# u of two tiles in one buffer of 640 columns, channel product with 64-row tails, new order of all work

## The chip, the cores and the metric

The kernel runs on one core of one Trainium2 chip. Five engines share its work: TensorE (PE in the profile, its weight loads PEld), VectorE (DVE), ScalarE (ACT), GpSimd (POOL) and SyncE (SP), which here only issues DMAs. The metric is the device time in microseconds (us), median of several runs. The profile is one execution, with its own time.

## The reference

Two layers. The first is a recurrence over 768 steps, for 4 batches of 8 heads with a state of 40 x 40 each; the second mixes its output over tokens and channels. Cut to what matters:

```python
for t in range(S):                                   # r, k, v, w, a, b: (4, 8, 768, 40)
    y[:, :, t] = einsum('bhd,bhde->bhe', r_t, state)
    Sa = einsum('bhde,bhe->bhd', state, a_t)
    state = state * w_t[:, :, None, :] - einsum('bhd,bhe->bhde', Sa, b_t) \
            + einsum('bhd,bhe->bhde', v_t, k_t)
x = y.transpose(0, 2, 1, 3).reshape(4, 768, 320)
theta = x @ w_theta                                  # (320, 320)
y = einsum('ts,bsd->btd', w_tok_r, x * cos(theta)) + einsum('ts,bsd->btd', w_tok_i, x * sin(theta))
u = x + y
out = u + maximum(u @ w_ch, 0)
```

## The kernel before, in words

The 768 tokens of a batch are six chunks of 128, so there are 24 tiles, 0 to 23, each of 128 tokens by 320 columns (8 heads of 40). Inside a tile the recurrence is done in closed form with products on PE; a state (`gt`) goes from tile to tile of a batch. Heads are padded from 40 to 64 columns, so that two heads fill 128 rows and a score product uses 64 rows of the array for each.

All work is written out by hand in a string, `ORDER`. An entry is a step, its tile, the engine that does it (A is ACT, V is DVE, G is POOL, S is a crossbar transpose by a DMA that SP issues) and, behind @, the PSUM place that it takes. `keep` holds each engine and queue to that order, so the string sets the order of PE, of each other engine, and of the DMAs of SP and POOL. The steps that the text speaks of:

- Loads: `LDW`, `LDR` (w and r of two tiles, 320 KB each), `LDK`, `LDB`, `LDA`, `LDV` (160 KB each), `LDT` (a row block of a token matrix, 192 KB), `LDC` (w_theta and w_ch).
- Decay: `LN` takes the logarithm of w of two tiles; `CSI` and `CSE` sum it over tokens with four 64-row products each, 320 wide (`pair_inc`, `pair_exc`); `CSE` goes on with nine small products for the totals. `INVW` and `WI` take the exponentials. `KH` and `AH` multiply k, b and a with them (tiles `kb`, `ah`).
- `TRK`, `TRA`, `TRR`, `TRV`, `NUT`, `GD` transpose on PE (`sm<-ident,...`), and `EKBT`, `EAT`, `ERT`, `EVT`, `ENUT`, `EGD` copy the result out of PSUM.
- Scores `PSI`, `PHI`, `LV`, `LU`: eight products of 64 rows each (`sc<-...`); `EPSI`, `EPHI`, `ELV`, `ELU` copy them with a mask on DVE, or without one on ACT, where POOL then masks (`MPSI` and so on).
- `X0`, `ENX`, `NU`, `ENU` solve for the tile's inner part; `GT`, `EGT` make the new state (`EGA` adds the old one on DVE, or `GI` does on PE); `Y`, `EX` make x.
- Second layer: `XT`, `EXT` transpose x (three chunks of 128 columns; x has 320, so the buffer of a tile is 384 wide with 64 columns of zeros), or `EXT:..S` does it with the crossbar; `TH` is three products with w_theta, `ETH` copies theta out where it is not read from PSUM, `SIN` takes both functions, `ZR` multiplies with x. `YR:i.j` adds the two token products of tile j of the batch to the sum of tile i. `EU` adds x, which gives u; `UT`, `EUT` transpose u in the same way as x; `CH` is three products with w_ch; `EO` takes max and adds u; `ST` stores.

PE's 3,266 products go through `mm` (line 278) and `transpose` (line 282), so these two lines, with the tiles' names, tell the steps apart in the profile. Copies go through line 270 (ACT) and line 272, products of two tiles through line 275. `EU` is line 705 and `EO` line 715. The first loads of tiles 0 and 1 that are marked A (`LDK:0A LDA:0A LDB:1A LDV:0A`) are issued by ACT's queue, the others by SP's; `LDT` and `LDC` by POOL's.

Of the kernel before, what the change touches and what calls it, by code (L numbers as in the profile page):

```python
# [10 lines left out]
FP32 = mybir.dt.float32  # L11
# [20 lines left out]
TRA:4@0 ELV:3A LDK:5 NU:3 TRK:4@3 LDB:5 GD:1@2 EAT:4V ENU:3A MLV:2G XT:0@0 EKBT:4V CR:4A GT:3@1
GI:3 EGD:1V EGT:3V PSI:4@1 EPSI:4V CV:4G PHI:4@0 LN:6A TRR:4@3 EPHI:4A NUT:3@2 MLV:3G Y:2@1
ENUT:3V LDB:6 LDA:6 AH:5G LDK:6 CSI:6@1 X0:4@2 EX:2V EXT:0A ERT:4A INVW:6A TRV:4@0 ENX:4V
MPHI:4G LDV:5 KH:5G LU:3@0 ERT:5A XT:1@1 NU:4 ELU:3V EXT:1A CSE:6@1 LDV:6 LDT:1.1G ENU:4A
TRA:5@3 WI:6A NUT:4@1 EVT:4V ENUT:4A TRK:5@2 LDK:7 EAT:5V AH:6G XT:2@0 EKBT:5V LV:4@0 TH:0@3
ELV:4V KH:6G PSI:5@1 GD:2@1 LDR:6 SIN:0A TH:1@2 LU:4@0 CV:5G GT:4@3 GI:4 EXT:2A EPSI:5V CV:6G
# [24 lines left out]
XT:7@2 EXT:7A LDB:14 LDT:3.1G ENX:11V TRA:12@3 LU:10@0 LV:11@1 ELU:10V NU:11 GD:9@0 EAT:12A
MLV:10G YR:1.0@2 ELV:11A LDA:14 TH:7@3 ENU:11V PSI:12@0 ETH:7A EGD:9V PHI:12@1 LDT:3.0G EPSI:12V
NUT:11@1 CV:12G KH:13G ENUT:11V YR:1.1 YR:1.2 SIN:7A WT:5.1@0 EPHI:12V YR:1.3 YR:1.4 X0:12@3
ENX:12A YR:1.5 MLV:11G EU:1V CR:12A Y:10@1 LDC:0.3G NU:12 EX:10V LU:11@0 LDK:14 AH:13G EWT:5.1V
SIN:6A TRV:12@2 TRR:12@1 ELU:11V EVT:12A TRK:13@0 EKBT:13V ERT:12A LDT:4.1G TH:8@2 ERT:13A
CSI:14@1 ZR:6G LDV:14 SIN:8A LV:12@0 LDW:16 YR:2.0@1 ELV:12V YR:2.1 TRA:13@0 EAT:13V CV:13G
# [6 lines left out]
LDV:15 NUT:13@3 EPSI:14V TRV:14@1 ENUT:13A CH:1@0 KH:15G EPHI:14A EO:1V TRR:14@2 TH:9@3 EVT:14V
ST:1 ERT:14V ETH:9A TH:10@0 AH:15G GT:13@1 LDR:16 MPHI:14G ETH:10A EGA:13V LDK:16 WT:4.0@3
EGT:13V EWT:4.0V LV:14@0 LU:13@1 TRK:15@0 EKBT:15V EGD:12S SIN:9A Y:12@1 YR:4.0@3 ELV:14V YR:4.1
YR:4.2 YR:4.3 LDT:5.0G ERT:15A TRA:15@0 CV:15G LDA:16 X0:14@2 ELU:13A YR:4.4 EAT:15V ENX:14V
YR:4.5 EU:4V SIN:10A XT:11@0 EXT:11V EX:12V PSI:15@0 MLU:13G PHI:15@1 EPSI:15A NU:14 TRV:15@3
LDB:16 UT:2@0 MPSI:15G EPHI:15V ENU:14A TH:11@1 LDW:18 CSE:16@0 EVT:15A LDV:16 EUT:2V GT:14@2
CSI:16@1 SIN:11A ZR:9G CR:16G CH:2@3 WT:5.0@0 EGA:14V EGT:14V Y:13@1 EO:2V ST:2 EWT:5.0V X0:15@2  # L80
ENX:15V NUT:14@3 WI:16A AH:16G EX:13V YR:5.0@0 YR:5.1 INVW:16A KH:16G YR:5.2 ENUT:14V LDK:17
NU:15 ENU:15V LV:15@0 LU:14@1 ELU:14V LN:18A TRA:16@1 EAT:16A UT:3@3 YR:5.3 LDB:17 LDA:17
NUT:15@2 CV:16G ZR:10G YR:5.4 EVT:16S ENUT:15V YR:5.5 TRK:16@1 EUT:3A EU:5V UT:4@3 CH:3@2
EKBT:16V TRR:16@0 EO:3V GD:13@1 EGD:13V KH:17G ELV:15A LDB:18 PHI:16@1 EPHI:16V PSI:16@0 EUT:4A
ST:3 GT:15@3 EPSI:16A MPSI:16G CH:4@2 LDV:17 Y:14@1 CSE:18@1 LDR:18 EO:4V ERT:16A EX:14V LDK:21
ERT:17A WI:18A TRK:17@2 EGA:15V EGT:15V AH:17G XT:13@1 UT:5@0 LV:16@0 EKBT:17A LU:15@1 EUT:5V
EXT:13V ZR:11G ST:4 ELU:15V X0:16@3 TRA:17@0 CH:5@1 YR:6.0@2 YR:6.1 ENX:16A ELV:16A NU:16 CV:17A
LDK:18 EAT:17V CSI:18@1 YR:6.2 ENU:16V LDA:18 XT:12@0 MLV:15G YR:6.3 EXT:12V EO:5V INVW:18A
PSI:17@0 PHI:17@1 EPSI:17A LDK:19 YR:6.4 GD:14@3 EPHI:17V TH:12@0 EGD:14A NUT:16@1 ENUT:16V ST:5
ETH:12A YR:6.5 LDV:18 MPSI:17G TRV:17@3 GT:16@0 EVT:17V Y:15@1 KH:18G EGA:16V LDA:19 SIN:12A  # L90
LV:17@0 EGT:16V LU:16@1 EX:15V EU:6V XT:14@3 EXT:14A AH:18G LDV:19 X0:17@0 TH:13@1 ENX:17A
MLV:16G LDW:20 TRK:18@2 LDB:19 SIN:13A YR:7.0@3 ELV:17V YR:7.1 YR:7.2 LDK:23 ELU:16V EKBT:18A
CV:18G TH:14@1 SIN:14A CR:18G YR:7.3 YR:7.4 TRA:18@2 YR:7.5 ZR:13G NU:17 ENU:17A EAT:18V
# [43 lines left out]
def kernel(  # L137
# [110 lines left out]
    def rows(p):  # L248
        return slice(64 * p, 64 * p + 64)
# [584 lines left out]
```

## Time and profile before

| what | us |
|---|---|
| median of 3 runs | 207.43 |
| lowest, highest | 206.94, 208.84 |
| time of the profiled execution | 206.92 |
| its span | 205.2 |
| first product of PE starts at | 6.20 |

The span runs from the first instruction to the last one's end. An instruction's row gives its start, its length, its engine and line, what it writes and reads, and how many were merged into the row; in square brackets stands how long its engine had been idle and what ended that. A group's row gives a count and a mean length in ns. Products on PE overlap: a row's length is a product's whole passage, and the distance between the starts of two rows is what PE spends on one.

### The profile page before, as it was taken

What the parts mean: (1) busy time and instruction counts of PE and PEld (TensorE: products, weight loads), DVE (VectorE), ACT (ScalarE), POOL (GpSimd) and SP (SyncE); (2) the same over time, 40 slices, a digit from 0 to 9 for tenths busy, and PEclk for the clock granted to TensorE, in tenths of its full rate; (3) what the DMA queues carried; (4) which work ended last, traced back from release to release, by engine and by line L of the source; (5) the groups of instructions that cost most, each with busy time, mean ns of one, the idle gap of its engine ahead of it and who ended that gap; (6) DMA issues with size and microseconds to landing.
All of it is one profiled execution on the core that took longest, in us unless ns stands there. A gap on an engine that the chain in (4) does not pass through costs nothing.

```text
span 205.2 us, 7809 instructions
## 1 busy us (share of the span) xinstructions
PE 190.1 (93%) x3266; PEld 147.5 (72%) x3266; DVE 170.6 (83%) x334; ACT 154.3 (75%) x259; POOL 147.1 (72%) x157
## 2 busy tenths in 40 slices
PE   0389999999999999999999999999999999999992
PEld 0166777877777887887887877887877787777671
DVE  7256899999999997999799998989888797975653
ACT  2367799997989997999899788987898685822100
POOL 8225778899989699998966886993989785634000
PEclk9999999999999999999999999999999999999999
DMA  7999999998898999899489989987979996433342
GB/s 136 187 240 159 225 171 178 173 230 140 153 221 154 213 159 216 164 213 226 103 171 193 192 172 238 192 135 161 169 97 154 218 129 140 99 90 103 102 150 96
DMA packets 144802, 34.17 MB, mean 167 GB/s; under 512 B 139520, under 2 KB 144768, under 8 KB 144768
## 3 DMA queue, kind: packets, MB, share of 16 engines
q1 hardware_dynamic: 138176, 30.26, 76.5%
q0 software_dynamic: 2432, 2.77, 8.4%
q10 hardware_dynamic: 4160, 0.66, 2.2%
q8 instruction: 25, 0.41, 0.9%
q14 instruction: 9, 0.07, 0.1%
HBM read 29.13 MB, written 3.93 MB: 161 GB/s over the span
## 4 chain that ended last, share of the span: by engine, by line
PE 80%; ACT 6%; DVE 5%; issue 2%; ACTq 2%; POOL 2%; POOLq 0%; DVEq 0%
PE sm L278 39%; PE sc L278 22%; PE sm L282 20%; ACTq L331 1%; ACT kbT L270 1%; ACT psi L270 1%; DVE phi L275 1%; ACTq L326 1%; ACT Wi_two L412 1%; ACT lw_two L338 1%; POOL z L275 1%; DVE lamu L275 1%; DVE rvT L272 1%; POOL lamv L554 1%; POOL phi L554 1%
## 5 line engine op out<-in xcount | busy, mean ns | idle before, releaser
L275 POOL TENSOR_TENSOR kb<-raw_kb,invW_two 128x640 bf16<-128x640 f32 x22 | 33.9, 1542 | 5.5 <-ACT invW_two L373 3.6
L275 POOL TENSOR_TENSOR z<-cs,x 128x640 bf16<-128x640 f32 x22 | 30.8, 1403 | 5.3 <-ACT cs L677 5.3
L278 PE MATMUL sm<-z,wtok_r 128*128 128x320 bf16 x120 | 34.3, 299 | 0.0
L278 PE MATMUL sm<-z,wtok_i 128*128 128x320 bf16 x120 | 34.2, 299 | 0.0
L275 POOL TENSOR_TENSOR ah<-raw_a,Wi_two 128x320 bf16<-128x320 f32 x22 | 19.0, 866 | 8.5 <-issue 5.2
L275 DVE TENSOR_TENSOR psi<-sc,mask_p 128x1024 bf16<-128x1024 f32 x16 | 19.5, 1219 | 1.0 <-PE sc L278 0.9
L554 POOL TENSOR_SCALAR_AFFINE_SELECT psi<-psi 128x1024 bf16<-128x1024 bf16 x8 | 8.7, 1093 | 14.0 <-ACT psi L270 11.6
L275 DVE TENSOR_TENSOR phi<-sc,mask_p 128x1024 bf16<-128x1024 f32 x14 | 17.1, 1219 | 1.6 <-PE sc L278 1.4
L278 PE MATMUL sc<-aT,kbT 64*128 64x128 bf16 x384 | 17.3, 225 | 1.1 <-ACT kbT L270 0.7
L275 DVE TENSOR_TENSOR lamu<-sc,mask_p 128x1024 bf16<-128x1024 f32 x14 | 17.1, 1220 | 0.6 <-PE sc L278 0.3
L282 PE MATMUL sm<-ident,kb 128*128 128x128 bf16 x184 | 14.9, 227 | 2.6 <-DVE kb L275 2.3
L278 PEld LDWEIGHTS <-wtok_r 128*128 128x128 bf16 x144 | 14.0, 97 | 4.6 <-issue 0.3
L270 ACT COPY rvT<-sm 128x512 bf16<-128x512 bf16 x28 | 15.9, 593 | 1.3 <-PE sm L282 0.7
L278 PEld LDWEIGHTS <-wtok_i 128*128 128x128 bf16 x144 | 14.1, 98 | 3.9 <-issue 0.2
L275 DVE TENSOR_TENSOR lamv<-sc,mask_p 128x1024 bf16<-128x1024 f32 x13 | 15.9, 1220 | 1.0 <-PE sc L278 0.5
L677 ACT ACTIVATE cs<-sm 128x320 f32<-128x320 f32 x26 | 9.9, 452 | 8.5 <-PE sm L278 8.4
L278 PEld LDWEIGHTS <-kbT 64*128 64x128 bf16 x384 | 11.9, 97 | 5.8 <-issue 2.4
L278 PEld LDWEIGHTS <-rvT 64*128 64x128 bf16 (+1 forms) x272 | 13.6, 95 | 2.9 <-issue 0.5
L278 PE MATMUL sm<-kb,lamv 128*128 128x40 bf16 x192 | 15.0, 180 | 0.0
L278 PE MATMUL sm<-kb,lamu 128*128 128x40 bf16 x192 | 14.9, 179 | 0.0
L282 PEld LDWEIGHTS <-kb 128*128 128x128 bf16 x184 | 11.5, 101 | 4.2 <-DVE kb L275 2.3
L554 POOL TENSOR_SCALAR_AFFINE_SELECT lamu<-lamu 128x1024 bf16<-128x1024 bf16 x10 | 10.9, 1090 | 4.1 <-ACT lamu L270 4.1
(137 smaller groups left out, 625.0 us busy)
## 6 DMA issues: line engine op xcount, KB each, us to landing
raw_w_two<-in_w_dram SPq DMA_DIRECT2D x12, 320.0 KB, 4.8
raw_r_two<-in_r_dram SPq DMA_DIRECT2D x12, 320.0 KB, 4.8
out_dram<-oo SPq DMA_DIRECT2D x24, 160.0 KB, 2.5
raw_kb<-in_b_dram SPq DMA_DIRECT2D x23, 160.0 KB, 4.6
raw_a<-in_a_dram SPq DMA_DIRECT2D x23, 160.0 KB, 4.5
raw_kb<-in_k_dram SPq DMA_DIRECT2D x23, 160.0 KB, 4.3
raw_v<-in_v_dram SPq DMA_DIRECT2D x23, 160.0 KB, 4.7
wtok_row<-in_moe_w_tok_r_dram POOLq DMA_DIRECT2D x6, 192.0 KB, 4.8
```

Source lines behind the costliest of these rows:

```text
L270: keep(nc.scalar.copy(out=out, in_=in_))
L272: keep(eng[e].tensor_copy(out=out, in_=in_))
L275: keep(eng[e].tensor_tensor(out=out, in0=in0, in1=in1, op=ALU.mult))
L278: keep(nc.tensor.matmul(out, lhsT=lhsT, rhs=rhs, start=start, stop=stop, skip_group_check=True))
L282: keep(nc.tensor.transpose(out=out, in_=in_, identity=ident))
L326: keep(queue[e].dma_start(out=tiles[i].raw_kb[:, j], in_=source(ap, i)))
L331: keep(queue[e].dma_start(out=t, in_=source(ap, i)))
L338: keep(nc.scalar.activation(out=q.lw[:, :, :, 0:D], in_=q.raw_w.rearrange("p h (j d) -> p j h d", j=2), func=AF.Ln))
L412: keep(nc.scalar.activation(out=two, in_=q.cse[:, LO:LO + 2 * DM + 16], func=AF.Exp))
L554: keep(nc.gpsimd.affine_select(out=flat, in_=flat, compare_op=ALU.is_ge, fill=0.0, base=-1, pattern=[[0, 2 * G], [1, 128]], channel_multip ...
L677: keep(nc.scalar.activation(out=cs[i % 5][:, c], in_=tiles[i].theta, func=AF.Sin, bias=(math.pi / 2, 0.0)[c]))
```

## The change

Five things change.

1. u of an even tile and of the next odd one lie in one buffer, 640 columns wide (`u_two`, three of them). The even tile's `UT` takes the chunks of columns 0 to 256 (two), the odd tile's those of 256 to 640 (three); the middle chunk has the last 64 columns of the even u and the first 64 of the odd u. The crossbar transposes two and three chunks likewise.
2. `CH` of a tile has two full products; the third, of 64 rows, goes to a step of its own, `CHR`, done once for a pair: rows 0 to 64 of the shared chunk end the even tile's sum, rows 64 to 128 begin the odd tile's. w_ch is held a second time, shifted by 64 rows (`wch` of five chunks instead of three), which takes two more loads, and `LDC` has new numbers. All 24 tiles are paired so. The code could pair x in the same way (`THR`), but the order has no such step.
3. `CST`, the nine small products for the totals, is a step of its own and no longer the end of `CSE`.
4. x lies in six buffers for two tiles each, still with its zeros; theta has three places instead of four; no load is issued by ACT.
5. The whole order is another one. Which engine does a copy changes in places; counts change from 14 to 15 `UT` on PE and 10 to 9 by the crossbar, 19 to 16 `XT` on PE and 5 to 8 by the crossbar, 11 to 12 `WT` on PE, 5 to 7 `GI` with 11 to 9 `EGA`.

The core of the diff; of the order only its first and last lines:

```diff
-LDW:0 LDK:0A LDB:0 LDA:0A LDA:1 LDB:1A LDK:1 LDV:0A LN:0A LDC:0.0G LDT:0.0G CSI:0@0 LDC:0.1G CSE:0@1 WI:0A
-INVW:0A KH:0V TRK:0@0 AH:0V EKBT:0A TRA:0@3 LDW:2 EAT:0V LDR:0 KH:1V PHI:0@1 PSI:0@0
...
-YR:21.4 YR:21.5 ST:19 CH:20@1 EU:21V YR:22.5 EO:20V YR:23.1 UT:21@0 EUT:21V ST:20 YR:23.2
-YR:23.3 YR:23.4 YR:23.5 EU:22V UT:22@1 CH:21@0 EU:23V EUT:22A EO:21V UT:23@3 CH:22@2 EUT:23V
-CH:23@1 EO:22V ST:21 EO:23V ST:22 ST:23
+LDW:2 LDT:0.0G LDW:0 LDB:0 LDC:0.0G LDT:0.1G LDK:0 LDK:1 LDT:1.0G LDC:0.2G LN:2A CSI:2@0 LDA:0
+LN:0A INVW:2A CSE:0@1 CST:0 CSI:0@0 INVW:0A WI:0A LDB:1 CSE:2@0 CST:2 KH:0V LDA:1 TRK:0@0
+EKBT:0A LDV:0 LDA:2 AH:0V TRA:0@3 LDK:2 KH:1V LDB:2 WI:2A EAT:0V PSI:0@1 AH:1V TRA:1@1 TRK:1@2
+CV:0A LDR:0 EPSI:0V EKBT:1A PHI:0@0 TRV:0@0 EAT:1V LDV:1 AH:2G X0:0@3 ENX:0A EPHI:0V PSI:1@1
+LDV:2 EPSI:1A PHI:1@0 NU:0 LDW:4 KH:2G EPHI:1V ENU:0A TRA:2@1 EAT:2A GT:0@2 EGT:0V EVT:0A LDK:3
+MPSI:1G CR:0A TRK:2@3 CV:1A GD:0@1 LDA:3 TRR:0@0 EKBT:2V ERT:0V PHI:2@1 LDB:3 X0:1@2 EPHI:2V
...
+LU:23@1 ELU:23V YR:17.2 YR:17.3 EUT:14S YR:17.4 Y:22@0 EUT:15S EX:22V YR:19.1 YR:17.5 YR:18.2
+EU:17V TH:21@1 EXT:22S Y:23@3 CH:14@0 ETH:21V EX:23V SIN:21A YR:19.2 YR:23.0@2 EXT:23S YR:23.1
+CHR:15@1 EO:14V CH:15 ZR:21G YR:20.0@1 EUT:17S YR:21.0 YR:21.1 TH:22@3 EO:15V YR:19.3 SIN:22A
+ZR:22G TH:23@0 YR:21.2 EUT:16S YR:23.2 ETH:23V YR:22.0@1 ST:14 YR:18.3 SIN:23A YR:20.1 YR:20.2
...
+YR:22.4 ST:19 YR:22.5 EO:18V UT:21@0 YR:23.4 EU:22V ST:18 YR:23.5 EUT:21A CH:20@3 CHR:21@1
+EU:23V UT:22@0 EO:20V UT:23@2 EUT:22V ST:20 CH:21 EUT:23V EO:21V ST:21 CH:22@3 CHR:23@0 EO:22V
+ST:22 CH:23 EO:23V ST:23
...
-    x_t = padded("x", [128, 3 * 128], 2 * NCH, lambda t: t[:, DM:])
-    u_t = padded("u", [128, 3 * 128], 3, lambda t: t[:, DM:])
+    u_two = [consts.tile([128, 2 * DM], BF16, name=f"u_two_{n}") for n in range(3 if twin_u else 0)]
+    def home(i, twins, one, two):
+        if i not in twins:
+            t = one[i % len(one)]
+            return t[:, 0:DM], t
+        t = two[i // 2 % len(two)]
+        if i % 2:
+            return t[:, DM:2 * DM], t[:, 256:2 * DM]
+        return t[:, 0:DM], t[:, 0:256]
...
-    th = mw.tile([128, 4, DM], FP32, name="th")
+    th = mw.tile([128, 3, DM], FP32, name="th")
-    wch = mw.tile([128, 3, DM], BF16, name="wch")
+    wch = mw.tile([128, 5 if twin_u else 3, DM], BF16, name="wch")
...
-        for kt in range(3):
+        for kt in range(src.shape[1] // 128):
             transpose(pt[:, kt * 128:kt * 128 + 128], src[:, kt * 128:kt * 128 + 128])
...
+    def mix(i, b, name, lhs, rhs, twins):
+        q = tiles[i]
+        if i not in twins:
+            setattr(q, name, bank(b))
+            for kt in range(3):
+                mm(getattr(q, name)[:, 0:DM], lhs[:, kt, :], rhs[:, kt, :], kt == 0, kt == 2)
+        elif i % 2 == 0:
+            setattr(q, name, bank(b))
+            for kt in range(2):
+                mm(getattr(q, name)[:, 0:DM], lhs[:, kt, :], rhs[:, kt, :], kt == 0, False)
+        else:
+            for kt in range(2):
+                mm(getattr(q, name)[:, 0:DM], lhs[:, 1 + kt, :], rhs[:, 3 + kt, :], False, kt == 1)
+
+    def mix_ends(i, b, name, lhs, rhs):
+        setattr(tiles[i], name, bank(b))
+        for c in range(2):
+            mm(getattr(tiles[i - 1 + c], name)[:, 0:DM], lhs[rows(c), 0, :], rhs[rows(c), 2, :],
+               c == 1, c == 0)
...
     def chan(i, b):
         q = tiles[i]
-        q.ops = bank(b)
-        mix3(q.ops[:, 0:DM], q.uT, wch)
+        mix(i, b, "ops", q.uT, wch, twin_u)
...
     def weight_load(n):
-        dst, src = ((wth, moe_w_theta), (wch, moe_w_ch))[n // 2]
+        dst, src = ((wth, moe_w_theta), (wch, moe_w_ch))[n // 4]
+        first, part = n % 2, n % 4 // 2
+        if part == 0:
+            keep(nc.gpsimd.dma_start(
+                out=dst[:, 3 * first:3 * first + 2, :],
+                in_=src[64 * first:64 * first + 256, :].rearrange("(a p) d -> p a d", p=128)))
+        else:
+            keep(nc.gpsimd.dma_start(out=dst[rows(first), 2, :],
+                                     in_=src[256 * (1 - first):256 * (1 - first) + 64, :]))
```

More of the change, by code (lines that the diff above doesn't have):

```diff
@@ L32 @@
[L32 to L37, printed above, removed]
@@ L62 @@
[L62 to L67, printed above, removed]
@@ L74 @@
[L74 to L91, printed above, removed]
```

260 lines of the change are left out of this document (145 added, 115 removed).

## The prediction

> **What bounds the kernel now.** I read the page first, then the stretches of 10 us, the waits of PE, and a piece of PE's own order.
>
> ```profile
> span 205.2 us, 7809 instructions
> PE 190.1 (93%) x3266; PEld 147.5 (72%) x3266; DVE 170.6 (83%) x334; ACT 154.3 (75%) x259; POOL 147.1 (72%) x157
> PE   0389999999999999999999999999999999999992
> PEclk9999999999999999999999999999999999999999
> PE 80%; ACT 6%; DVE 5%; issue 2%; ACTq 2%; POOL 2%; POOLq 0%; DVEq 0%
> ```
>
> PE is busy 93% of the span and carries 80% of the chain that ended last. It is idle only at the two ends, and the granted clock shows no loss. The stretches and PE's waits say the same:
>
> ```profile
> 0.00:10.00 10.00, 1.59 (x17) 0.90 (x17) 5.05 (x47) 3.33 (x4) 5.53 (x17) 1.00 1.05 161
> 10.00:20.00 10.00, 8.71 (x100) 6.69 (x100) 5.82 (x10) 7.03 (x11) 3.72 (x3) 1.00 1.20 207
> 20.00:30.00 10.00, 9.38 (x198) 7.22 (x194) 8.78 (x13) 7.92 (x13) 6.98 (x9) 1.00 1.01 197
> 40.00:50.00 10.00, 9.85 (x200) 7.98 (x198) 9.89 (x17) 9.51 (x18) 9.55 (x12) 1.00 0.95 181
> 100.00:110.00 10.00, 10.00 (x170) 8.15 (x164) 9.63 (x17) 9.28 (x16) 7.25 (x9) 1.00 0.79 151
> ```
>
> ```profile
> PE sc L278 <- ACT lw_two L338: 6.5, 2, 6.2
> PE sm L282 <- DVE kb L275: 2.3, 1, 2.3
> ```
>
> Columns of the stretches: length, busy time of PE, PEld, DVE, ACT and POOL, granted clock, DMA share, GB/s. From 40 us on PE is full, so there a product that goes is time gained; between 40 and 50 us DVE, ACT and POOL are nearly full too, so an eviction added there would cost. Before 30 us PE waits, for the first logarithm and for the first kb, and runs slowly: 100 instructions in its second stretch, 198 in the third. There the loads and the chain of the first tiles decide.
>
> **What a product costs PE.** A busy row shows a product's whole passage. What it costs in a full PE is the time until the next one starts, which a piece of PE's order shows:
>
> ```profile
> 109.53 0.30 PE L278 MATMUL sm<-z,wtok_r 128*128 128x320 bf16 x1
> 109.67 0.30 PE L278 MATMUL sm<-z,wtok_i 128*128 128x320 bf16 x1
> 109.81 0.33 PE L282 MATMUL sm<-ident,x 128*128 128x128 bf16 x3
> 110.07 0.62 PE L278 MATMUL sc<-aT,kbT 64*128 64x128 bf16 x16
> 110.62 0.37 PE L278 MATMUL sm<-nx,phi 128*128 128x40 bf16 x8
> ...
> 111.06 0.33 PE L282 MATMUL sm<-ident,u 128*128 128x128 bf16 x3
> 111.22 0.57 PE L278 MATMUL sm<-wth,xT 128*128 128x320 bf16 x3
> 111.73 0.45 PE L278 MATMUL sc<-lw_two,pair_exc 64*128 64x320 bf16 x4
> 112.11 0.18 PE L278 MATMUL sc<-off_two,ident 128*128 128x16 bf16 x1
> ```
>
> A product 320 wide takes 0.14 (109.53 to 109.67), a transpose 0.053 (three from 111.06 to 111.22). The three theta products should be through at 111.22 + 3 x 0.135 = 111.63, but the 64-row products behind them start at 111.73: going over to 64 rows costs 0.10. The four 64-row products, 320 wide, are followed at 112.11, 0.38 later: two pairs side by side (2 x 0.135) and 0.11 for going back. So a lone visit to 64 rows costs about 0.2 for its two changes, and a pair of tails another 0.135. The Trainium skill says the same of the change ("TensorEngine Tiling (Array Packing)", Key Properties: "Mode switching requires drain", changing the tiling mode drains TensorE). By that rule alone, with every tail a lone visit, a pair of tails would cost 0.34 against 0.27 for the two full products that it replaces, a loss of about 0.8 us over 12 pairs; the trace agrees with the drain.
>
> **What PE's list loses and gains** (counted in the two orders, entry by entry). Channel product: 72 products become 48 full ones and 12 pairs of tails, 72 x 0.1355 = 9.8 before, 48 x 0.1355 + 12 x 0.133 = 8.1 after: -1.7. Transposes of u on PE 42 to 39, of x 57 to 48, of the token rows 66 to 72: -6 x 0.055 = -0.3. The product that adds the old state (GI) 5 to 7: +0.3. Changes between 128 and 64 rows: 167 before, 153 after, though 12 tails came in. Seven of the 12 CHR stand beside other 64-row products, and CST, split from CSE, lets CSE and CSI stand together. -14 x 0.10 = -1.4. In all -3.1 us of PE's time, none of it hidden by other work. Up to the end of the last token product (YR:23.5) it is -3.5, because more channel work is left for the end.
>
> **The end.**
>
> ```profile
> 199.35 0.30 PE L278 MATMUL sm<-z,wtok_i 128*128 128x320 bf16 x1
> 199.69 0.49 DVE L705 TENSOR_TENSOR u<-sm,x 128x320 bf16<-128x320 f32 x1 [0.33 <-PE sm L278]
> 200.67 0.35 DVE L272 COPY uT<-sm 128x384 bf16<-128x384 bf16 x1
> 201.69 0.49 DVE L715 SCALAR_TENSOR_TENSOR oo<-sm,u 128x320 f32<-128x320 f32 x1
> ```
>
> The last token product is through at T = 199.35 + 0.14 = 199.49; the last output (EO:23) starts on DVE at T + 2.2. After the change DVE has EU:23, EO:20, EUT:22, EUT:23 one after another: T + 0.2 + 0.49 + 0.49 + 0.35 + 0.35 = T + 1.88. Then PE does the tails of 22 and 23 (CHR:23, which waits for uT of 23), two changes and two products of CH:23, while EO:22, which cannot start before CHR:23 has closed its sum, is queued on DVE ahead of EO:23: tails through at T + 2.2, EO:22 T + 2.4 to 2.9, EO:23 at T + 2.9. That is +0.7.
>
> **Late crossbar transposes.** The crossbar transposes x eight times now (five before) and u nine times (ten).
>
> ```profile
> xT<-x SPq DMA_TRANSPOSE x4, 3.2
> ```
>
> That is the median from issue to landing in us, from 120 us on. The chain Y:23, EX:23, EXT:23, TH:23 went over PE; now EXT:23 goes over SP's queue. Between Y:23 and TH:23 lie 3.2 us of PE's work; the chain needs 0.2 + 0.49 + 3.2 = 3.9. +0.6 or 0.7 is late, bounds 0 (other stalls ahead give the time) and 2 (two transposes queued ahead on SP, and behind them EUT:17 and EUT:16, which CH:17 and CH:16 wait for). I take +0.6.
>
> **The head.** Before, tile 0's w goes first, and four loads of tiles 0 and 1 go by ACT's queue. After, all go by SP's, w of tile 2 ahead of w of tile 0, and three token rows by POOL's instead of one.
>
> ```profile
> GB/s 0 0 0 0 17 87 184 288 285 261 240 231 184 179 183 182 181 184 180 181 184 203 189 199 196 195 198 215 281 286 296 305 278 262 236 214 186 168 177 168
> ```
>
> ```profile
> 5.41 0.74 ACT L338 ACTIVATE lw_two<-raw_w_two 128x640 bf16<-128x640 f32 x1 [3.33 <-DMA raw_w_two<-in_w_dram]
> 9.17 0.83 DVE L275 TENSOR_TENSOR kb<-raw_kb,invW_two 128x640 bf16<-128x640 f32 x1 [3.76 <-ACT invW_two L373]
> 10.05 1.04 PE L282 MATMUL sm<-ident,kb 128*128 128x128 bf16 x8 [2.26 <-DVE kb L275]
> 17.31 0.63 SPq L331 DMA_DIRECT2D raw_a<-in_a_dram  x1
> 23.95 0.86 POOL L275 TENSOR_TENSOR ah<-raw_a,Wi_two 128x320 bf16<-128x320 f32 x1
> ```
>
> The first line is the rate in slices of 0.4 us from the start. The two w are 655 KB; at 285 from about 2.3 us on they have landed by 4.7, so LN:0 can start near 5.0, though LN:2 is ahead of it on ACT, and everything behind up to the first kb keeps its lengths: near 8.6 instead of 9.17, -0.5 (bounds -1, if the four w-sums of both tiles are out of the way before PE is wanted, and +0.7, LN:2's length, if w of 0 lands late). The prices come later: tile 3's last input is 864 KB (0.88 MB) further back, at the 197 GB/s of the third stretch 4.5 us. Its cover: a of tile 3 was issued at 17.31 and is wanted at 23.95; with the page's median landing
>
> ```profile
> raw_a<-in_a_dram SPq DMA_DIRECT2D x23, 160.0 KB, 4.5
> ```
>
> it lay ready 2.1 us, and TRK:3 stands 2.1 us of PE's work later in the new list. 4.5 - 4.2 leaves +0.3, bounds 0 and 4.5.
>
> **The other engines.** DVE has 289 entries with an operand of its own in both orders, ACT 221 and 220, POOL 143 and 146 (a z, a mask, a cast and two weight loads more, two casts of v fewer), against 35, 51 and 58 us that they have free. In the first 50 us of PE's work, where the row of 40 to 50 us shows no free DVE, DVE has 86 entries instead of 89, so I cost the moves at nothing; three more there would be 1.5 us, since PE follows DVE in that stretch. The two added loads of w_ch (200 KB, 1 us of DMA at 197) go by POOL's queue long before the first CH. The theta buffer has three places instead of four, and in the list each is read by SIN before ETH writes it again.
>
> **The sum.** 205.2 - 3.5 + 0.7 + 0.6 - 0.5 + 0.3 = 202.8 of span. The profiled execution took 206.92, 1.7 more than its span, and lay 0.5 under the median of 207.43: 202.8 + 1.7 + 0.5 = 205.0.
>
> **Rivals.**
> *The head starves, slower.* One cause, the order of the loads: w of tile 0 lands late behind w of tile 2 (+0.7 instead of -0.5), and the 4.5 us by which tile 3's inputs come later lie on the path whole: 205.0 + 1.2 + 4.2 = 210.4. For it: the DMA share stands at 1.0 or above in each stretch to 30 us, so nothing can catch up. Against it: PE's waits name no DMA, and the new list has TRK:3 2.1 us later. From 2.4 us of such waits on nothing is gained, from 4.5 on it is slower by over 1%. 0.14.
> *The gain goes into the new waits, no change.* Two crossbar transposes queue ahead of EXT:23 and EUT:16 (+2 instead of 0.6), and three evictions come late where DVE is full, half of their 1.5 us hidden: 205.0 + 1.4 + 0.7 = 207.1. For it: those engines are full. Against it: a count of all places where a result is wanted by PE within half a us of its earliest end gives 75 in the old order and 77 in the new after 20 us, so the new list is no tighter. 0.14.
> *The tails don't run side by side.* Then each pair takes 0.27: +1.6, 206.6. Against it: the four 64-row products above, 0.38 with a change. 0.03.
> *PE starts and warms earlier.* The eight transposes at 10.05 take 1.04; at 0.053 apart they would take 0.6 (seven steps and the last one's passage of 0.22): the early products run at about half rate. The first w-sums may start when the first w is in, some 1.5 us sooner than now; if all behind follows by that much instead of 0.5, and the fast rate saves another 1.0, 203.0. The Trainium skill has this rule ("TensorE: Matmul & The Clock Gate", Part 1: full rate after about 3.4 us of sustained activity); the granted clock of 1.00 in the first stretches does not show it, the product spacing does. 0.11.
>
> **Chances and range.** The forecast has 0.58, with its own range of 203.9 to 206.4 (the bounds of the crossbar, -0.6 and +1.4, and half a us of the first kb below). 1% either way (205.36 and 209.50) is about what a measurement of this kernel tells from no change. Of the forecast 0.44 lies below 205.36 and 0.14 above. Faster: 0.44 + 0.11 = 0.55. Same: 0.14 + 0.14 + 0.03 = 0.31. Slower: 0.14. The range of 203.0 to 208.8 leaves out the starved head and half of the early start.
>
> **What would show it.** Right: PE's busy rows of the channel product fall from 72 to about 48 full ones and 24 of 64 rows, tails 3 to 5 ns apart; PE full from 40 us on; TH:23 preceded by a short wait for a DMA; about 2.9 us between the last token product and the last output. Wrong: a wait of PE for kb or ah before 35 us that ends in a DMA (the starved head), gaps of PE spread over 40 to 150 us (a tighter list), or a first kb later than 9.2.

## The result and the profile after

| what | before | after |
|---|---|---|
| median, us (16 runs each, same chip) | 207.72 | 209.80 |
| ratio, with its 95% interval | 1 | 1.0096 (1.0071 to 1.0121) |
| span of the profiled execution | 205.2 | 209.1 |
| first product of PE starts at | 6.20 | 4.90 |
| last product of PE starts at | 201.36 | 205.23 |

Ratios, here and below, are of fast executions alone: some executions of a kernel are slower, mostly at a lower granted clock, and the profiled ones of two kernels below are such ones, g1's (clock 0.58), which therefore has no gaps in the table, and f1's (1.7% above its fastest).

205.0 was forecast, from 203.0 to 208.8: the changed kernel is 1% slower and outside the range. The page of the profile after, first the span, PE's busy time, its busy tenths in 40 slices, and the chain that ended last by engine:

```profile
span 209.1 us, 7804 instructions
PE 188.3 (90%) x3262; PEld 145.5 (70%) x3262; DVE 169.3 (81%) x331; ACT 153.4 (73%) x258; POOL 150.6 (72%) x160
PE   0718989989999999998999999999999999898992
PE 69%; DMA 12%; DVE 5%; ACT 5%; SPq 2%; issue 2%; POOL 1%; DVEq 0%; POOLq 0%
```

PE is busy 1.8 us less (188.3 against 190.1) in a span that is 3.9 us longer, and DMA, which had no share of the chain before, now has 12%. The slices say where: the third (10.5 to 15.7 us) has a 1, and of the last six, which were full before but for the last, two have an 8. The stretches, with the columns of the prediction's:

```profile
0.00:10.00 10.00, 3.75 (x39) 1.92 (x40) 4.93 (x43) 4.66 (x6) 6.59 (x19) 1.00 0.94 170
10.00:20.00 10.00, 4.88 (x58) 3.81 (x56) 4.70 (x7) 3.40 (x5) 0.86 (x1) 1.00 0.96 172
20.00:30.00 10.00, 8.61 (x149) 6.42 (x146) 8.39 (x13) 8.31 (x16) 6.36 (x6) 1.00 1.05 200
40.00:50.00 10.00, 9.43 (x191) 7.67 (x188) 9.11 (x20) 9.41 (x16) 8.61 (x10) 1.00 1.01 193
190.00:200.00 10.00, 8.64 (x65) 5.50 (x65) 4.66 (x10) 1.59 (x4) 2.73 (x2) 1.00 0.36 109
```

In the second stretch PE did 58 products, where before did 100. In that from 190 us it is busy 8.64 us, where before had 9.96. What it waited for (total, times, longest):

```profile
PE sc L297 <- ACT lw_two L357: 5.4, 2, 4.9
PE sm L301 <- DVE ah L294: 4.3, 1, 4.3
PE sm L297 <- DMA xT<-x_two: 1.0, 1, 1.0
PE sc L297 <- DMA rvT<-v: 0.9, 1, 0.9
PE sc L297 <- DVE aT L291: 0.8, 1, 0.8
PE sm L297 <- DMA uT<-u_two: 0.4, 1, 0.4
```

The wait for kb of 2.3 us is gone. A wait for ah of 4.3 us is new, and so are waits for three crossbar transposes.

To account for the whole difference I use one sum from the trace: from each product's start to the next one's, less the slot that the product takes in a full PE (those of the prediction, and 0.094 us for a change of rows), is a **gap**. Summed over all products, gaps were 17.1 us before and are 25.3 after:

| part, us | before | after | difference |
|---|---|---|---|
| start to first product | 6.20 | 4.90 | -1.3 |
| products and changes of rows (what remains without gaps) | 178.1 | 175.1 | -3.0 |
| gaps up to 30 us | 10.0 | 13.9 | +4.0 |
| gaps from 30 to 170 us | 6.2 | 7.0 | +0.8 |
| gaps from 170 us on | 0.9 | 4.3 | +3.5 |
| last product to the end | 3.8 | 3.9 | 0.0 |

The sum is 205.2 to 209.1. The row of the products is what remains, so it is the counted list at these slots by construction; whether the slots are right has to be read from the starts themselves, which is done at the end. Against the list's 3.0 us the gaps at the two ends have 7.5.

**The first gap.** ah of tile 0 is DVE's product of `raw_a` and `Wi_two`. Rows of DVE, of SP's queue (start, length of the issue) and of POOL's loads in the profile after:

```profile
8.64 0.83 DVE L294 TENSOR_TENSOR kb<-raw_kb,invW_two 128x640 bf16<-128x640 f32 x1 [3.35 <-ACT invW_two L392]
14.38 0.49 DVE L294 TENSOR_TENSOR ah<-raw_a,Wi_two 128x320 bf16<-128x320 f32 x1 [4.91 <-DMA raw_a<-in_a_dram]
```

```profile
5.02 0.72 SPq L350 DMA_DIRECT2D raw_a<-in_a_dram  x1
5.78 3.60 SPq L345 DMA_DIRECT2D raw_kb<-in_b_dram  x1
9.43 1.75 SPq L350 DMA_DIRECT2D raw_a<-in_a_dram  x1
```

```profile
4.25 0.71 POOL L760 DMA_DIRECT2D wtok_row<-in_moe_w_tok_r_dram  x1
...
6.74 0.56 POOL L785 DMA_DIRECT2D wth<-in_moe_w_theta_dram  x1
```

kb comes at 8.64, as forecast. Then DVE waits 4.9 us for a load of 160 KB that was issued at 5.02 and was there at 14.4, 9.3 us later; before, this load was issued by ACT's queue and ah ran at 9.91. From 4.25 to 7.30 us POOL issued five loads. What each queue moved from 5 to 13 us (packets, MB, and the time that its packets took as a share of the 16 DMA engines' time), after:

```profile
q0 software_dynamic: 775, 0.79, 61.7%
q1 hardware_dynamic: 4761, 0.75, 59.8%
```

and before, where q10 is ACT's queue:

```profile
q1 hardware_dynamic: 3843, 0.85, 62.2%
q10 hardware_dynamic: 2821, 0.44, 41.6%
q0 software_dynamic: 496, 0.40, 31.0%
```

q0 is POOL's queue, q1 SP's. Before, the two queues with the tiles' inputs moved 1.29 MB in these 8 us; after, the only one left moved 0.75 MB, beside twice as much of POOL's.

**The last gaps.** The chain that ended last, around 180 and 190 us, and three rows of SP's queue:

```profile
177.25 4.46 DMA rvT<-v
181.71 0.04 issue
181.75 0.40 PE sc L297 x8
...
188.18 4.23 DMA xT<-x_two
192.41 0.05 issue
192.46 0.58 PE sm L297 x3
...
193.39 2.28 DMA uT<-u_two
```

```profile
177.25 1.21 SPq L518 DMA_TRANSPOSE rvT<-v  x1
185.59 2.50 SPq L679 DMA_TRANSPOSE uT<-u_two  x2
188.18 3.80 SPq L679 DMA_TRANSPOSE xT<-x_two  x2
```

The transpose for rvT takes 4.5 us from its issue to the products that need it, the first of x, which is tile 22's, 4.2; an issue holds SP's queue for 1.2 us or more. The piece at 188.18 starts right behind two transposes of u, and the three products at 192.46 are `TH:22`, which waited for it. `TH:23`, at 193.15, waited for nothing.

### The profile page after: what moved, and what is told of

Its sections match the earlier page's. It is cut to its first block, busy times and chain, and to the rows that moved or that the text cites. A ratio compares the mean times of both kernels' runs of the same rounds, so it can differ in the third digit from the quotient of the medians.

```text
span 209.1 us, 7804 instructions
## 1 busy us (share of the span) xinstructions
PE 188.3 (90%) x3262; PEld 145.5 (70%) x3262; DVE 169.3 (81%) x331; ACT 153.4 (73%) x258; POOL 150.6 (72%) x160
## 4 chain that ended last, share of the span: by engine, by line
PE 69%; DMA 12%; DVE 5%; ACT 5%; SPq 2%; issue 2%; POOL 1%; DVEq 0%; POOLq 0%
PE sm L297 33%; PE sm L301 18%; PE sc L297 18%; DMA raw_kb<-in_b_dram 4%; DMA wtok_row<-in_moe_w_tok_i_dram 3%; DMA rvT<-v 2%; DMA xT<-x_two 2%; SPq L345 1%; DVE lamv L294 1%; DMA uT<-u_two 1%; ACT rvT L289 1%; DVE rvT L291 1%; POOL z L294 1%; ACT L715 1%; DVE phi L294 1%
## 5 line engine op out<-in xcount | busy, mean ns | idle before, releaser
L294 POOL TENSOR_TENSOR z<-cs,x_two 128x640 bf16<-128x640 f32 x23 | 32.2, 1404 | 13.7 <-ACT cs L715 11.0
L297 PE MATMUL sc<-aT,kbT 64*128 64x128 bf16 x384 | 18.1, 225 | 1.7 <-DVE aT L291 0.8
L294 DVE TENSOR_TENSOR lamv<-sc,mask_p 128x1024 bf16<-128x1024 f32 x15 | 18.3, 1220 | 1.5 <-PE sc L297 1.0
L294 DVE TENSOR_TENSOR psi<-sc,mask_p 128x1024 bf16<-128x1024 f32 x15 | 18.3, 1217 | 1.0 <-PE sc L297 0.9
L294 DVE TENSOR_TENSOR phi<-sc,mask_p 128x1024 bf16<-128x1024 f32 x14 | 17.1, 1219 | 1.7 <-PE sc L297 1.5
L294 DVE TENSOR_TENSOR lamu<-sc,mask_p 128x1024 bf16<-128x1024 f32 x12 | 14.6, 1217 | 2.8 <-PE sc L297 2.7
L576 POOL TENSOR_SCALAR_AFFINE_SELECT lamu<-lamu 128x1024 bf16<-128x1024 bf16 x12 | 13.1, 1090 | 3.8 <-ACT lamu L289 3.8
L289 ACT COPY rvT<-sm 128x512 bf16<-128x512 bf16 x24 | 14.0, 601 | 2.1 <-PE sm L301 1.7
L297 PE MATMUL sm<-wth,xT 128*128 128x320 bf16 x72 | 13.7, 299 | 1.4 <-DMA xT<-x_two 1.0
L715 ACT ACTIVATE cs<-th 128x320 f32<-128x320 f32 x26 | 10.6, 472 | 5.4 <-DVE th L291 5.4
L291 DVE COPY rvT<-sm 128x512 bf16<-128x512 bf16 x22 | 12.6, 575 | 2.1 <-ACT rvT L289 1.1
```

Of the source, the lines that this page charges most:

```text
L289: keep(nc.scalar.copy(out=out, in_=in_))
L291: keep(eng[e].tensor_copy(out=out, in_=in_))
L294: keep(eng[e].tensor_tensor(out=out, in0=in0, in1=in1, op=ALU.mult))
L297: keep(nc.tensor.matmul(out, lhsT=lhsT, rhs=rhs, start=start, stop=stop, skip_group_check=True))
L576: keep(nc.gpsimd.affine_select(out=flat, in_=flat, compare_op=ALU.is_ge, fill=0.0, base=-1, pattern=[[0, 2 * G], [1, 128]], channel_multip ...
L715: keep(nc.scalar.activation(out=cs[i % 5][:, c], in_=tiles[i].theta, func=AF.Sin, bias=(math.pi / 2, 0.0)[c]))
```

## The experiments

Times are compared by the ratio to the kernel before on the same chip; 0.1% is 0.2 us. The gaps are of the profiled execution of each; the expectations call them PE's excess.

| kernel | ratio to before (95%) | gaps to 30 us | gaps from 170 us |
|---|---|---|---|
| before | 1 | 10.0 | 0.9 |
| the changed kernel | 1.0096 (1.0071 to 1.0121) | 13.9 | 4.3 |
| e1 two token rows of POOL later | 1.0025 (0.9986 to 1.0064) | 11.3 | 3.8 |
| e2 raw_a ahead of k of tile 1 | 1.0080 (1.0049 to 1.0112) | 13.0 | 3.0 |
| e3 late transposes on PE | 1.0051 (1.0030 to 1.0073) | 13.3 | 2.4 |
| e4 e1 and e3 | 0.9980 (0.9960 to 1.0000) | 11.7 | 1.8 |
| f1 pairs in the old order | 1.0473 (1.0387 to 1.0559) | 10.1 | 6.9 |
| f2 new order, no pairs | 1.0155 (1.0062 to 1.0247) | 12.9 | 3.9 |
| f3 all five loads of POOL later | 0.9956 (0.9908 to 1.0003) | 9.3 | 3.5 |
| f4 f3, e2 and e3 | 0.9951 (0.9923 to 0.9978) | 9.8 | 1.6 |
| g1 f3 and e3 | 0.9936 (0.9907 to 0.9965) | - | - |
| g2 g1 without pairs | 1.0047 (1.0015 to 1.0079) | 9.4 | 3.0 |
| g3 before, POOL's loads later | 1.0033 (1.0011 to 1.0055) | 10.3 | 1.0 |
| g4 before, two token rows earlier | 1.0071 (1.0046 to 1.0097) | 10.4 | 1.2 |

### e1 to e4: the two ends, one at a time

e1 moves two of the five early loads of POOL behind later work of POOL:

```diff
-LDB:0 LDC:0.0G LDT:0.1G LDK:0 LDK:1 LDT:1.0G LDC:0.2G LN:2A CSI:2@0 LDA:0
+LDB:0 LDC:0.0G LDK:0 LDK:1 LDC:0.2G LN:2A CSI:2@0 LDA:0
...
-LV:3@0 KH:5G
+LV:3@0 KH:5G LDT:1.0G
...
-ERT:6A ZR:1G
+ERT:6A ZR:1G LDT:0.1G
```

> The changed kernel with two of the three early token rows (LDT:0.1 and LDT:1.0) moved back in POOL's order to where tiles 5 and 6 are prepared; all else as it is. Theory 1 (POOL's rows hold up SP's loads in the first 14 us, so a of tile 0 lands at 14.4 instead of about 9.5): the first ah starts near 10, PE's wait of 4.3 us for it shrinks to under 1, and the time falls by 2.5 to 4 us, to 206 to 207. Rival (it is the place of LDA:0 in SP's own order, behind two w, two k and a b): the first ah starts later than 13 and the time falls by less than 1 us.

e2 leaves POOL alone and puts the load that was late one place ahead on SP's queue (the two entries with a G are POOL's):

```diff
-LDK:0 LDK:1 LDT:1.0G LDC:0.2G LN:2A CSI:2@0 LDA:0 LN:0A
+LDK:0 LDA:0 LDK:1 LDT:1.0G LDC:0.2G LN:2A CSI:2@0 LN:0A
```

> The changed kernel with LDA:0 moved up in SP's order by one place, ahead of LDK:1; POOL's rows stay where they are. Theory 1: a of tile 0 comes a little sooner (11 to 13), but k of tile 1 and all behind it are held up by the rows as before, and the time falls by less than 1.5 us. Rival (SP's order): the first ah starts near 9.5 and the time falls by 2.5 us or more.

e3 takes three transposes from SP's queue and gives them to PE, with a copy by ACT or DVE:

```diff
-EO:12V EVT:23S YR:16.0@2 YR:16.1 EO:13V YR:16.2
+EO:12V YR:16.0@2 YR:16.1 EO:13V YR:16.2 TRV:23@0 EVT:23A
...
-EU:17V TH:21@1 EXT:22S Y:23@3
+EU:17V XT:22@0 EXT:22V TH:21@1 Y:23@3
...
-YR:23.0@2 EXT:23S YR:23.1
+YR:23.0@2 YR:23.1 XT:23@3 EXT:23V
```

> The changed kernel with three of its late crossbar transposes (v of tile 23, x of tiles 22 and 23) done on PE and copied by DVE and ACT instead; ten transposes more on PE, 0.55 us. Theory 2 (after 170 us PE waits for crossbar transposes that queue on SP and land 4 us later): the gaps of PE after 170 us, 4.3 us in the changed kernel, fall to 2 or less, and the time falls by 1.5 to 2.5 us, to about 207.8. Rival (the gaps are those of a tighter order of DVE and would come anyway): gaps stay above 3.5 us and the time is the same within 0.7 us.

> Both edits, the token rows later and the three late transposes on PE. Theory 1 and 2 together: the two gains add up, 4 to 6 us, to 204 to 206, below the kernel before. If the two were one cause, or if PE's list were not really 3 us shorter, the time stays at 207 or above.

The row of ah in e1 (DVE):

```profile
12.04 0.49 DVE L294 TENSOR_TENSOR ah<-raw_a,Wi_two 128x320 bf16<-128x320 f32 x1 [2.53 <-DMA raw_a<-in_a_dram]
```

2.3 us sooner than in the changed kernel, but not near 10: half of what was expected, and so is the time, 0.7% or 1.5 us where 2.5 to 4 were. In e2 ah ran at 9.70, about where the rival put it, but that brought next to nothing, 0.16% with intervals that overlap, where the rival had 2.5 us. Two rows of e2 say why, of DVE and of PE's waits:

```profile
14.52 0.83 DVE L293 TENSOR_TENSOR kb<-raw_kb,invW_two 128x640 bf16<-128x640 f32 x1 [4.32 <-DMA raw_kb<-in_b_dram]
```

```profile
PE sc L296 <- DVE aT L290: 4.7, 1, 4.7
```

Now DVE waits for b of tile 1, with aT of tile 0 queued behind it, and PE waits for aT. The wait moved one load further on. So it is not that one load stood at the wrong place; all of SP's loads were slow in these microseconds.

e3 gains 0.45% (0.9 us; 1.3 by the medians), less than the 1.5 to 2.5 us expected, for gaps at the end that are 2.0 us shorter and three steps that PE now does itself, by the slots 0.6 us. From 170 us on no wait of PE for a DMA is left in its profile. e4 is faster than the changed kernel by 1.15%, against 0.70% and 0.45% alone: the two gains add. But that is 2.4 us, and 4 to 6 were expected. Its gaps from 170 us on are 1.8, and a gap of 0.6 us that stands just behind 170 us in e3 stands just before it here.

### f1, f2: the pairing and the order apart

f1 is the order of before, loads by ACT included, with the pairing alone; the two `CH` of a pair stand together, here the first pair:

```diff
-CH:0@1
-EO:0V EWT:3.0V ST:0 CSE:14@0
+EWT:3.0V CSE:14@0 CST:14
...
-CH:1@0
+CH:0@2 CHR:1@0 EO:0V CH:1 ST:0
```

> The pairing alone: the order of work of the kernel before (its loads on ACT's queue too), with u of two tiles in 640 columns, five chunks transposed per pair, the 64-row tails side by side. Each pair's channel products stand together where the later of the two stood, and uT has 3 buffers in place of 2, or two open pairs would block each other. Counted with the slots of the prediction, TensorE's list is 160.4 us of products where before had 162.5, but the pairs bring 191 mode changes where before had 167: at 0.094 us each the sum is 178.4 us against 178.2. Theory 1 (the pairing is worth its product slots less the mode changes; the loss of the changed kernel is in its new order): about 207.7 us, the same as before, within 0.7. Rival (mode changes around the tails cost nothing, since the tails run side by side): 205.6, 2.1 less. Second rival (the pairing itself loses, by waits for u of both tiles): 208.5 or more, with new idle time of PE at the lines of the channel product.

f2 is the changed kernel with u unpaired:

```diff
-CHR:1@1
+CH:1@1
...
-CH:1
```

> The new order alone: the changed kernel with its order and loads, but u of each tile in a buffer of its own again (6 of them), three chunks transposed per tile and three 128-row products per tile; the tails' 64-row products are gone. Counted with the slots, TensorE's list is 176.4 us where the changed kernel has 175.2 (145 mode changes against 153). Theory 1 (order: head starved and late crossbar; the pairing gains its slots): 1.2 us slower than the changed kernel, 211.0. Rival (the pairing is what made the end late, since the last uT waits for two tiles): 208.5 or less, with the crossbar waits after 170 us down from 4.3 us to 2.

In f1 u of tile 13 was transposed ahead of that of tile 12, as the old order has it, so tile 12's tail multiplies columns of another u; no instruction is missing for that. It is 4.7% slower, far from both 207.7 and 205.6 and on the side of the second rival. The three largest of PE's waits after 40 us:

```profile
PE sm L298 <- POOL kb L291: 2.4, 3, 2.1
PE sm L298 <- DVE oo L749: 1.9, 6, 0.6
PE sm L294 <- DVE oo L749: 1.0, 3, 0.6
```

The waits for `oo` are for a PSUM place, since a pair holds two of the four until both `EO` are done. I put that down to the placing, which was not tuned; no run shows it, and these three rows are 5.3 us of a loss of 9.8. So f1 does not tell what the pairing costs in that order. What it does tell is the price of a change of rows. Around its 12 pairs of tails, each a lone visit, the next product starts 0.094 to 0.096 us late going over (once 0.130) and 0.107 coming back, which makes 2.4 us for the 24 changes and eats the 2.1 us of products that the pairing saves. So a rival by which these changes cost nothing falls, and an order that puts tails beside other 64-row products is part of the gain.

f2 is 0.6% slower than the changed kernel, the 1.2 us of the slots, though with a wide interval. The rival's 208.5 would be a ratio of 1.004, below f2's whole interval: the loss of the changed kernel is not in the pairing.

### f3, f4: POOL's loads all out of the way

```diff
-LDW:2 LDT:0.0G LDW:0 LDB:0 LDC:0.0G LDT:0.1G LDK:0 LDK:1 LDT:1.0G LDC:0.2G LN:2A
+LDW:2 LDW:0 LDB:0 LDK:0 LDK:1 LN:2A
...
-AH:4G
+AH:4G LDT:0.0G
...
-MLU:2G
+MLU:2G LDC:0.0G
...
-LV:3@0 KH:5G
+LV:3@0 KH:5G LDT:1.0G
...
-ERT:6A ZR:1G
+ERT:6A ZR:1G LDT:0.1G
...
-ZR:0G
+ZR:0G LDC:0.2G
```

> The changed kernel with all five early loads of POOL's queue (three rows of the token weights, both parts of the theta weights) moved behind work of POOL after 20 us; nothing else. Theory 1 (POOL's 0.7 MB squeeze SP's loads between 5 and 13 us): the first ah, at 14.38 us in the changed kernel and at 12.04 with two of the five moved, comes at about 10; PE's excess of the first 30 us falls from 13.9 to about 10.3 and the time by 2 to 3 us, to 207 to 208. Rival (SP's own queue is too long at the start, one queue where before had two): ah stays near 12 and the time at 208.8, that of the run with two rows moved.

f4 adds e2 and e3, and copies aT of tile 0 ahead of kb of tile 1:

```diff
-LDB:0 LDK:0 LDK:1 LN:2A CSI:2@0 LDA:0
+LDB:0 LDK:0 LDA:0 LDK:1 LN:2A CSI:2@0
...
-KH:1V LDB:2 WI:2A EAT:0V PSI:0@1
+LDB:2 WI:2A EAT:0V KH:1V PSI:0@1
```

> All together: POOL's five early loads moved as in the run beside it, raw_a of tile 0 loaded ahead of k of tile 1 and aT of tile 0 copied before kb of tile 1 is scaled, and the late crossbar transposes (vT of tile 23, xT of tiles 22 and 23) on TensorE. Theory 1: 3 us from the head, 1.3 from the end: 205.0 to 206.0, 1.7 to 2.7 below the kernel before. Rival (the head's gain is taken up again by what waits next): 207, as with the two rows moved and the same end.

In these two, theta of tiles 0 to 2 is made before the second part of its weights is loaded, so it lacks the last 64 channels; no instruction is left out. f3, in the order of the fences of the changed kernel above (DVE, SP's queue, and the queues from 5 to 13 us):

```profile
9.40 0.48 DVE L294 TENSOR_TENSOR ah<-raw_a,Wi_two 128x320 bf16<-128x320 f32 x1
```

```profile
5.06 1.05 SPq L350 DMA_DIRECT2D raw_a<-in_a_dram  x1
6.16 0.67 SPq L345 DMA_DIRECT2D raw_kb<-in_b_dram  x1
6.87 0.71 SPq L350 DMA_DIRECT2D raw_a<-in_a_dram  x1
```

```profile
q1 hardware_dynamic: 9105, 1.43, 116.5%
```

ah waits for nothing: DVE goes from kb to ah without a pause. The same load of b that took SP 3.60 us to issue takes 0.67, and SP's queue moves 1.43 MB where it moved 0.75, in the same order of loads (packets in flight together count each for itself, so a share can pass 100%). Gaps up to 30 us fall by 4.6 to 9.3, and the kernel gains 1.4%, 2.9 us, on the changed one; not all of the 4.6 reaches the time, since the gaps between 30 and 170 us grow by 2.6 in its profile. Theory 1 holds; the rival, one queue where before had two, falls. f4 is no faster than f3 by more than the intervals, and its gaps up to 30 us are no shorter: with POOL quiet, the place of `LDA:0` is worth nothing. Its ratio gives 206.7, the rival's 207 and not theory 1's 205.0 to 206.0, and the gain of e3 is not to be seen in it beyond the intervals.

### g1 to g4: the parts put together, and the cross-check in the old kernel

g1 is f3 and e3, with both parts of the theta weights at `MLU:2G`; g2 is g1 with the edit of f2. g3 and g4 are the kernel before:

```diff
 g3
-LDC:0.0G LDT:0.0G CSI:0@0 LDC:0.1G
+CSI:0@0
...
-MPSI:3G
+MPSI:3G LDC:0.0G LDC:0.1G
...
-AH:4G
+AH:4G LDT:0.0G
 g4
-LDC:0.0G LDT:0.0G CSI:0@0 LDC:0.1G
+LDT:0.0G LDC:0.0G LDT:0.1G CSI:0@0 LDT:1.0G LDC:0.1G
```

> The changed kernel with POOL's five early loads moved behind work of POOL after 20 us (both parts of the theta weights together this time, ahead of the first theta) and the late crossbar transposes (vT of tile 23, xT of tiles 22 and 23) on TensorE; raw_a and kb keep the changed kernel's order. Theory 1 (two independent causes, whose shares add): the gain of POOL's loads alone, 2.3 us against the changed kernel, and of the end alone, 1.3 us, together 3.6: 206.1 where before gives 207.7, ratio 0.992. Rival (the head's gain is lost again at the next wait): 207, as the kernel with raw_a also moved.

> The same kernel without the pairing: u of each tile by itself, three chunks transposed per tile, three 128-row products per tile, no 64-row tails. By the slots TensorE's list is 1.2 us longer. Theory 1 (the pairing gains its slots less its mode changes, and the loss of the changed kernel was all in its order): 1.2 us slower than the kernel beside it, 207.3. Rival (in a kernel without the head's gaps the pairing costs waits on u of both tiles): the same or faster than the kernel beside it, 206.1 or less.

> The kernel before with its three early loads of POOL's queue (a row of the token weights, both parts of the theta weights) moved behind work of POOL after 20 us. In it a of tile 0 was issued by ACT at 1.35 us, ahead of POOL's traffic, and the first ah at 9.9 us waits for nothing that a DMA does. Theory 1 (POOL's traffic costs only where it stands ahead of loads that PE waits for): no change, 207.7 within 0.5. Rival (it costs wherever it runs early): 206.5.

> The kernel before with two more rows of the token weights (0.39 MB) in POOL's early loads, as the changed kernel has them: five loads at the head of POOL's queue. Theory 1 (POOL's traffic squeezes the loads of SP and ACT that run beside it): loads of tiles 1 to 3 come late, and PE's excess of the first 30 us grows from 10.0 to about 12 us, the time to about 209. Rival (it was the changed kernel's order of loads on one queue, not POOL's traffic): no change, 207.7 within 0.5.

g1 measured 206.3 us (206.1 was expected), 1.6% below the changed kernel and 0.64% (0.35 to 0.93) below the one before: the lowest ratio of all, though not clear of e4, f3 and f4, and with f4 one of two that are below 1 with their whole interval.

g2 is 1.1% slower than g1, 2.3 us, where the slots gave 1.2. The rest can be looked for in its profile, beside that of f4, which has the same end: its gaps are 1.2 us longer. One row of PE's waits is nearly all of that, a crossbar transpose of a single u that took 4.5 us, where most take 2.4 (more on that below):

```profile
PE sm L296 <- DMA uT<-u: 1.0, 1, 1.0
```

g3 shows that moving POOL's loads is no gain by itself: in the kernel before it lost 0.3%, hardly more than nothing. Before's a was loaded ahead of them, so nothing of PE waited for what they slowed. g4 costs 0.7%, 1.5 us, about the time of theory 1, but not at its place. The queues from 5 to 13 us are as expected:

```profile
q0 software_dynamic: 667, 0.72, 52.0%
q1 hardware_dynamic: 2551, 0.44, 43.3%
q10 hardware_dynamic: 2471, 0.39, 36.7%
```

The tiles' inputs get 0.83 MB where they had 1.29. Yet the gaps up to 30 us grow by only 0.5 us, against the 2 expected; the other 1.9 of the 2.4 in its profile lie later, 0.8 of them between 50 and 60 us. So in this kernel too POOL's rows took from the queues beside them; how dear that is seems to depend on which load stands in it, and at this head it was only those 0.5 us. The later 1.9 us no run took apart.

## Why the prediction was wrong, step by step

**PE's list: right, as far as it can be read.** -3.1 was forecast, and the list counted with the slots gives -3.0. The form rows have the products of the channel product as counted:

```profile
L297 PE MATMUL sm<-wch,uT x72: 295/300/311, 105.7 to 205.2; 128*128 128x320 bf16 x48, 64*128 64x320 bf16 x24
```

The price of a change of rows held too, read from the starts on its two sides, less the slot of the product before it: the median is 0.096 us in each of five kernels with 145 to 191 changes (before, after, f1, f2, f4), where the sum had 0.10. By the Trainium skill ("TensorEngine Tiling (Array Packing)", Key Properties) a change of the tiling mode drains TensorE; f1 agrees, where the 24 more changes cost about 2.4 us for the 2.1 us of products saved.

**The end: right in size.** Rows of DVE at the end: `EU:23`, and the last three `EO`.

```profile
203.04 0.49 DVE L743 TENSOR_TENSOR u_two<-sm,x_two 128x320 bf16<-128x320 f32 x1 [0.22 <-PE sm L297]
204.71 1.37 DVE L752 SCALAR_TENSOR_TENSOR oo<-sm,u_two 128x320 f32<-128x320 f32 x3
```

The last token product is through 0.2 before 203.04, at 202.84; the last `EO` ends at 204.71 + 1.37 = 206.08 and so starts at 205.59, 2.75 us after it. 2.9 was forecast and 2.2 stood before: +0.55 where the sum had +0.7.

**Late crossbar transposes: the right kind of wait, at another place and far too small.** The step priced one chain, from `Y:23` to `TH:23`, at +0.6 and let it go to 2 with a queue. That wait did not come; `TH:22`, one tile earlier, waited 1.0. And the gaps from 170 us on grew by 3.5; the named waits there are 2.7 in all, 2.3 for crossbar results and 0.4 for a copy of rvT by DVE. What the step left out: it looked at the transposes that were moved to SP's queue, not at those that were there already, and gave them one time, the median of 3.2. `EVT:23S` stood in the old order too. There it took 2.4 us from issue to landing (the first row below, a view of before), here 4.5, and PE waited 0.9 for it; in e1 it took 2.3 again, and PE did not wait. The second row, in the page of after, is the queue that loads instructions (packets, MB, share):

```profile
rvT<-v SPq DMA_TRANSPOSE x1, 2.4
q8 instruction: 25, 0.41, 0.8%
```

A packet of 16 KB of this queue starts at 179.15, within the 4.5 us, and the next one at 189.41, within the 4.2 us of tile 22's x. With 2.4 us both results would have been there before PE had done the products ahead, at 180.7 and 191.3. That the packets are the cause was not tried by a run of its own, but if they are, a part of this loss is luck in where they fall. e3 shows that the three transposes of tiles 22 and 23 are the cause of most of the loss, 2.0 us of gaps.

**The head: the step that failed.** "-0.5" for kb was right (8.64 where 8.6 was forecast), and so was the earlier first product. "+0.3", for tile 3's inputs, looked for the price some 10 us too late. The sentence "three token rows by POOL's instead of one" told what the change did, and the sum then gave it no term: the working took the order of loads on SP's queue for the supply, as if that queue had the DMA engines to itself. What the runs showed in its place: POOL's 0.79 MB halve what SP's queue moves from 5 to 13 us (0.75 against 1.43 MB in f3), the load of a, which stands in the middle of it, takes 9.3 us, and it costs 4.6 us of gaps up to 30 us (13.9 against f3's 9.3). The page of before held a warning: there too POOL's queue moved 0.40 MB between 5 and 13 us. There a of tile 0 had been issued by ACT ahead of it, at 1.35 us, and g3, which takes that traffic away, gains nothing.

The Trainium skill has the rule that the step left out ("DMA: Bandwidth & Descriptors", Issuing engines are not separate DMA queues: transfers of all issuing engines run on the same 16 DMA engines and interleave; its section Queues, rings and completion order adds that each engine takes turns between queues, packet by packet). The traces agree: with POOL's queue quiet SP's moves 1.9 times as much. The turns themselves no run here shows.

**The rivals.** The starved head, 0.14, gave 210.4, nearest to the 209.8 measured, and what would show it (a wait of PE for ah that ends in a DMA) is what the profile shows. Its cause was only half named: not w of tile 0 behind that of tile 2, and not tile 3, but the loads beside SP's queue. "PE starts earlier" came true by 1.3 us and was worth nothing, since the next load was late. The tails run side by side: the two products of a pair start 2 to 4 ns apart in the trace of after. Of the tighter list there is little: +0.8 us of gaps between 30 and 170 us, spread over many places, where 0.7 + 1.4 had been the rival's price together with the crossbar; no run took it apart.

**The sum.** -3.0 (list), -1.3 (first product), +4.0 (head), +0.8, +3.5 (end): +3.9 before rounding, where the forecast had -2.4. With the two mistakes of order taken away the change is worth about half of what was expected of it: g1, which keeps the pairs and the rest of the order, is 0.64% faster than before, 1.3 us (0.7 to 1.9) where the forecast had 2.4.

## What to carry to other kernels

When loads are moved, count the bytes of every queue in the same microseconds, not the places on one: ask which load that an engine waits for stands beside the new traffic. When a list gets shorter, each asynchronous result that was just in time becomes late; look at the transposes that did not move, too. And a pairing that brings narrower products has to be placed beside others of their kind, or its changes of rows take the gain.

## What the runs showed of the hardware that had not been expected

Issuing a load is not a fixed price: the same entry of SP's queue took 0.67 us with POOL's queue quiet and 3.60 beside it, and the loads behind it were issued that much later. A crossbar transpose near the end mostly holds SP's queue for 1.2 us and lands 2.3 to 2.4 us after its issue, but some take up to 4.5, where the DMA share of a stretch was 0.35 to 0.46, so a full DMA does not explain them. Of 185 transposes after 170 us, in the profiles of all kernels but g1, 48 took more than 2.5 us, and each of these overlaps a packet of the instruction queue; of the 124 that overlap none, none took more than 2.41. Not every overlap is slow, and no run tried these packets by themselves. And the packets of POOL's loads have 1,019 bytes on average (0.79 MB in 775) where SP's have 158 (0.75 MB in 4,761), which may be why 0.79 MB of them weigh so much; that was not tried by itself.
